# Copying the next expert's first weights ahead of the residual sum, and issuing the weight transfers from the fourth attention step on

## The chip, the cores and the metric

The kernel runs on one core of one Trainium2 chip. The metric is device time in microseconds (us) of one execution. A difference of about 2% is what a measurement of this kernel can tell from none.

## The reference

Attention in chunks of 32 queries feeds a layer of eight experts. Only what matters is shown:

```python
# attention: B, H, S, D = 4, 8, 768, 64; per chunk of 32 queries: 8 memory keys + 16 left + 32 own + 8 right
scores = scale * np.matmul(q_c, k_full.transpose(0, 1, 3, 2))
a = np.exp(scores - np.max(scores, axis=-1, keepdims=True))
a = a / (np.sum(a, axis=-1, keepdims=True) + 1e-09)
out[:, :, c_start:c_end] = np.matmul(a, v_full)
...
# experts: x is [3072, 512]; w1, w2 are [8, 512, 512]
h_dense = np.maximum(x @ w1_dense, 0.0)
y_dense = h_dense @ w2_dense
expert_idx = np.argmax(x @ w_gate, axis=1)
gate_w = probs[np.arange(N), expert_idx]
for e in range(E):
    mask = expert_idx == e
    h = np.maximum(x[mask] @ w1[e], 0.0)
    y_moe[mask] = gate_w[mask, None] * (h @ w2[e])
return (y_dense + y_moe).astype(np.float32)
```

## The kernel before

The work has three stages, one after the other. The instructions of each engine stand in the order in which the code writes them; waits between engines are put in by the framework from the tiles that they share.

**Attention** (loop over `g`, line 392). 24 tiles of 128 queries run through a software pipeline of 28 steps: step `g` does the scores of tile `g`, the transposes of tile `g-1`, the values of tile `g-2` (line 257, reading `vw`), and the gate logits of tile `g-4`. The values come in eight halves of 12 chunks each (`load_v`, lines 139 to 166), many small transfers on SyncE's queue (SP), into three buffers in turn; half `n` serves tiles `3n` to `3n+2`. Queries and keys (`kb`, `qb`, line 135) come by GpSimd's queue (POOL). POOL also casts each tile into its row (line 269) and, once per group of three tiles, scatters the rows to a list per expert in memory, `xs` (line 342). `load_w` (line 75) sends the next of 18 weight transfers on POOL's queue: two for the dense layer, then two for each of eight experts, each 512 KB as it lands in `wall`. Before the change it is called in steps 14 to 27, and four more times in the first steps of the dense stage (line 543).

**Dense stage** (loop at line 540). After a short table of VectorE (DVE) arithmetic, which ends in the row numbers `rowi` (line 466), POOL gathers the 128 tokens of each of 31 slots out of `xs` into `xg` (`fetch`, line 482), three slots ahead. TensorE (PE) transposes them (`turn`, line 492, tile `xt`), and does both dense products: `first` (line 503, 16 matmuls into `ph`, then ReLU into `h` on ScalarE, ACT) and `second` (line 513, four matmuls into `py`). The dense result of a slot is kept in `yds`.

**Expert stage** (loop at line 567). A slot `j` belongs to one expert, whose number is known only at run time. `bring(j)` (line 522) copies that expert's weights to a fixed place: the first weights `wa` on DVE (line 529), half of the second weights `wb` on DVE (line 531) and half on ACT (line 533). Both tiles have two buffers. PE then does `first(j)` with `wa` and `second(j-1)` with `wb`. `finish(j-1)` (line 553) computes the residual sum `o = py * gate + yds` on DVE (line 556) and scatters it to the output on POOL (line 558).

The order in the expert loop is written by hand: PE gets `first(j)`, `second(j-1)`; DVE gets the sum of slot `j-1`, then the copies `wa` and `wb` of slot `j+1`.

Of the kernel before, what the change touches and what calls it, by code (L numbers as in the profile page):

```python
# [11 lines left out]
BF16 = mybir.dt.bfloat16  # L12
# [15 lines left out]
DT, FT = DM // 128, F // 128  # L28
# [4 lines left out]
NSLOT = NT + E - 1  # L33
# [8 lines left out]
def kernel(  # L42
# [14 lines left out]
    nc = tc.nc  # L57
# [9 lines left out]
    wall = const.tile([128, E + 1, DT + FT, 512], BF16, name="wall")  # L67
# [39 lines left out]
    with ExitStack() as one:  # L107
# [75 lines left out]
        def transposes(b, sink):  # L183
            qT = qt_p.tile([128, HP, S], BF16, tag="qT", name=f"qT{b}")
            kbd = kbds[b % 2]

            def step(hp, isk):
                src = qk.pop((b, hp, "kb" if isk else "qb"))
                tp = ps.tile([128, TPB, 128], BF16, tag="ps", name="tp")
                for i in range(TPB):  # L190
                    for par in range(2):
                        nc.tensor.transpose(tp[64 * par:64 * par + 64, i, :],  # L192
                                            src[:, par, D * i:D * i + D], ident,
                                            tile_position=(0, 64 * par))
                tv = tp.rearrange("d i p -> d p i")
                if not isk:
                    nc.scalar.copy(qT[:, hp, :].rearrange("d (p i) -> d p i", i=TPB), tv)
                    load_qk()
                else:
                    for par in range(2):  # L200
                        r = slice(64 * par, 64 * par + 64)
                        dst = kbd[r, hp, par, LEFT:LEFT + S].rearrange("d (p i) -> d p i", i=TPB)
                        nc.scalar.copy(dst, tv[r])  # L203

            for hp in range(HP):
                sink.append(lambda hp=hp: step(hp, True))
                sink.append(lambda hp=hp: step(hp, False))
            return qT, kbd
# [84 lines left out]
        def new_group(n):  # L293
            grp = grps[n]
            grp["row"] = work.tile([128, GRP, ROW], F32, tag="row", name="row")
            grp["pg"] = pg.tile([128, 2, GRP, E], F32, tag="pg", name="pg")
            nc.gpsimd.tensor_copy(
                grp["row"][:, :, DM // 2 + 1].bitcast(I32), tok[:, GRP * n:GRP * n + GRP])
# [93 lines left out]
        for g in range(NT + 4):  # L392
            def do(part, lag):
                if 0 <= g - lag < NT:
                    parts[g - lag][part]()

            if g < NT:
                b, t = divmod(g, TPB)
                if t == 0 and b + 1 < B:
                    steps = []  # L400
                    turned[b + 1] = transposes(b + 1, steps)
                parts[g] = attention(g, *turned[b], grps.setdefault(g // GRP, {}))
            do("scores", 0)
            do("turn", 1)
            if 0 <= g - 2 < NT and (g - 2) % GRP == 0:
                new_group((g - 2) // GRP)
            do("values", 2)
            do("exp", 0)
            if g < NT and t > 0 and steps:
                steps.pop(0)()  # L410
            do("turn_x", 3)
            if g < NT and t > 2 and steps:
                steps.pop(0)()
            do("gate", 4)
            if g >= 14:
                load_w()
            if g % 3 == 1 and g > 3 and g // 3 + 2 < 2 * B:
                load_v(g // 3 + 2)
# [51 lines left out]
    with ExitStack() as two:  # L470
        c2 = two.enter_context(tc.tile_pool(name="c2", bufs=1))
        w2 = two.enter_context(tc.tile_pool(name="w2", bufs=2))
        w3 = two.enter_context(tc.tile_pool(name="w3", bufs=4))
        pt = two.enter_context(tc.tile_pool(name="pt", bufs=2, space=PSUM))
        pf = two.enter_context(tc.tile_pool(name="pf", bufs=3, space=PSUM))
        xTs = c2.tile([128, NSLOT, DT, 128], BF16, name="xTs")
        yds = c2.tile([128, NSLOT, DM], F32, name="yds")
        meta = c2.tile([128, NSLOT, 2], F32, name="meta")

        xgs = {}  # L480

        def fetch(j):
            if j >= NSLOT:
                return
            xg = w3.tile([128, ROW], F32, tag="xg", name="xg")
            nc.gpsimd.indirect_dma_start(  # L486
                xg.bitcast(I32), None, xs[:, :],
                bass.IndirectOffsetOnAxis(ap=rowi[:, j:j + 1], axis=0),
                bounds_check=ZROW, oob_is_err=True)
            xgs[j] = xg  # L490

        def turn(j):
            if j >= NSLOT:
                return
            xg = xgs.pop(j)
            xt = pt.tile([128, DT, 128], BF16, tag="xt", name="xt")
            xb = xg[:, :DM // 2].bitcast(BF16)
            for d in range(DT):
                nc.tensor.transpose(xt[:, d, :], xb[:, 128 * d:128 * d + 128], ident)  # L499
            nc.vector.tensor_copy(xTs[:, j], xt)  # L500
            nc.vector.tensor_copy(meta[:, j, :], xg[:, DM // 2:DM // 2 + 2])

        def first(j, w):
            ph = pf.tile([128, FT, 128], F32, tag="ph", name="ph")
            for f in range(FT):
                for d in range(DT):
                    nc.tensor.matmul(ph[:, f, :], w[:, d, 128 * f:128 * f + 128],  # L507
                                     xTs[:, j, d, :], start=(d == 0), stop=(d == DT - 1))
            h = w2.tile([128, FT, 128], BF16, tag="h", name="h")
            nc.scalar.activation(h, ph, AF.Relu)  # L510
            return h

        def second(h, w):
            py = pf.tile([128, DM], F32, tag="py", name="py")
            for f in range(FT):
                nc.tensor.matmul(py, h[:, f, :], w[:, f, :],  # L516
                                 start=(f == 0), stop=(f == FT - 1))
            return py

        hs, regs, copied = {}, {}, {}  # L520

        def bring(j):

            if j >= NSLOT:
                return
            ev, ea = regs[j]
            wa = w2.tile([128, DT, 512], BF16, tag="wa", name="wa")
            wb = w2.tile([128, FT, 512], BF16, tag="wb", name="wb")
            nc.vector.tensor_copy(  # L529
                wa, wall[:, bass.ds(ev, 1), :DT].rearrange("p a t m -> p (a t) m"))  # L530
            nc.vector.tensor_copy(
                wb[:, :2], wall[:, bass.ds(ev, 1), DT:DT + 2].rearrange("p a t m -> p (a t) m"))
            nc.scalar.copy(  # L533
                wb[:, 2:], wall[:, bass.ds(ea, 1), DT + 2:].rearrange("p a t m -> p (a t) m"))
            copied[j] = (wa, wb)

        for j in range(3):
            fetch(j)
        turn(0)
        for j in range(NSLOT + 1):  # L540
            if j < NSLOT:
                fetch(j + 3)
                load_w()
                hs[j] = first(j, wall[:, E, :DT])
                turn(j + 1)
                regs[j] = (nc.vector.value_load(expi[:1, j:j + 1], min_val=0, max_val=E - 1),
                           nc.scalar.value_load(expi[:1, j:j + 1], min_val=0, max_val=E - 1))
            if j > 0:
                nc.scalar.copy(yds[:, j - 1], second(hs.pop(j - 1), wall[:, E, DT:]))

        sent = []

        def finish(j, wb, h):
            py = second(h, wb)
            o = w3.tile([128, DM], F32, tag="o", name="o")
            nc.vector.scalar_tensor_tensor(o, py, meta[:, j, 0:1], yds[:, j],  # L556
                                           op0=ALU.mult, op1=ALU.add)
            i = nc.gpsimd.indirect_dma_start(  # L558
                out[:, :], bass.IndirectOffsetOnAxis(ap=meta[:, j, 1:2].bitcast(I32), axis=0),
                o, None, bounds_check=NT * 128 - 1, oob_is_err=False)  # L560
            for x in sent:
                tc.declare_no_dep(i.ins, x.ins, reason="different rows of out")
            sent.append(i)

        bring(0)
        bring(1)
        for j in range(NSLOT + 1):
            if j < NSLOT:
                hs[j] = first(j, copied[j][0])
            if j > 0:  # L570
                finish(j - 1, copied[j - 1][1], hs.pop(j - 1))
                bring(j + 1)

# [28 lines left out]
```

## Time and profile before

| what | value |
|---|---|
| three timed runs | 399.64, 406.48, 406.95 us; median 406.48 us |
| the profiled execution | 393.16 us, of which its span is 391.5 us |
| PE busy in the span | 275.8 us (70%) |
| DVE, ACT, POOL busy in the span | 155.9, 169.0 and 147.9 us (40%, 43%, 38%) |
| attention, dense stage, expert stage | until about 201 us; about 208 to 283 us; about 283 us to the end |

All times in the profile are in microseconds from the start of the span, of one execution. An instruction's row gives its start, its length, its engine, its line and its tiles, and in square brackets how long the engine was idle before it and what ended that idle time. PE's matmuls are pipelined: a row of sixteen matmuls shows 1.06 us, while the next group starts 0.89 us after it. PEclk is the granted clock of TensorE: 1.00 is 2.4 GHz, 0.50 is 1.2 GHz.

### The profile page before, as it was taken

The page shows a single profiled execution, that of the slowest core. Times are in us where ns is not written, and L with a number is a line of the kernel's source. Part 1 is how long each engine was busy: PE and PEld are TensorE (multiplying, and loading weights), DVE is VectorE, ACT ScalarE, POOL GpSimd, SP SyncE. Part 2 cuts the span into 40 slices and gives each one's busy share as a digit, 9 for nine tenths or more (in the row PEclk, how much of TensorE's full clock was granted, in tenths as well). Part 3 has the DMA queues.
Part 4 walks back from the last instruction along what each step waited for, and adds up shares of the span by engine and source line. Part 5 has one row for each costly group of instructions (what it writes and reads, how often), then busy time and mean ns, then how long its engine had stood idle before and what let it go on. Part 6 is the DMA issues. An engine that isn't in the chain of part 4 may idle for free.

```text
span 391.5 us, 10333 instructions
## 1 busy us (share of the span) xinstructions
PE 275.8 (70%) x4200; PEld 206.4 (53%) x4200; DVE 155.9 (40%) x432; ACT 169.0 (43%) x253; POOL 147.9 (38%) x183
## 2 busy tenths in 40 slices
PE   2604778788979798889830879999955555555553
PEld 1403567676858576678830657777633333333331
DVE  7104343552444434354352212222435544444553
ACT  3704365364525444233200335555665555444442
POOL 8751321313032231516263845555023333333333
PEclk9999986785556658565555799999999999999999
DMA  8999998995907799875788892223101211221110
GB/s 105 195 188 176 156 172 131 180 153 121 124 32 120 119 141 174 136 105 91 129 139 158 145 199 62 70 70 66 19 28 71 81 64 68 75 79 62 67 59 0
DMA packets 74193, 42.40 MB, mean 108 GB/s; under 512 B 53439, under 2 KB 70848, under 8 KB 74146
## 3 DMA queue, kind: packets, MB, share of 16 engines
q0 software_dynamic: 23616, 29.33, 38.6%
q1 hardware_dynamic: 50530, 12.41, 20.8%
q8 instruction: 33, 0.54, 0.6%
q14 instruction: 14, 0.11, 0.1%
HBM read 48.02 MB, written 11.30 MB: 152 GB/s over the span
## 4 chain that ended last, share of the span: by engine, by line
PE 41%; issue 25%; POOL 10%; DMA 9%; SPq 7%; DVE 4%; ACT 1%; another core or an unknown queue 1%; POOLq 1%; ACTq 0%
POOL out_dram L558 9%; PE xp L257 7%; PE pg L282 7%; PE ph L507 6%; SPq L164 5%; PE xtp L275 5%; PE py L516 5%; PE ap L245 5%; PE tp L192 3%; DMA vw<-in_v_dram 3%; DMA xg<-xs,rowi 3%; DMA vw<-in_mem_v_dram 2%; PE sc L224 2%; SPq L159 2%; DMA xs<-row,si 2%
## 5 line engine op out<-in xcount | busy, mean ns | idle before, releaser
L510 ACT ACTIVATE h<-ph 128x512 bf16<-128x512 f32 x62 | 36.9, 597 | 74.5 <-PE ph L507 73.8
L558 POOL DMA_INDIRECT out_dram<-o,meta x31 | 35.8, 1155 | 78.8 <-DVE o L556 75.2
L507 PE MATMUL ph<-xTs,wa 128*128 128x128 bf16 x496 | 32.9, 220 | 42.0 <-DVE wa L529 42.0
L507 PEld LDWEIGHTS <-wa 128*128 128x128 bf16 x496 | 27.9, 98 | 56.5 <-DVE wa L529 56.3
L269 POOL CAST row<-xn 128x512 bf16<-128x512 f32 x24 | 14.7, 611 | 80.5 <-DVE xn L266 80.5
L556 DVE SCALAR_TENSOR_TENSOR o<-py,meta,yds 128x512 f32<-128x512 f32 x31 | 23.3, 751 | 53.5 <-PE py L516 49.2
L486 POOL DMA_INDIRECT xg<-xs,rowi x31 | 31.8, 1025 | 32.5 <-PE py L516 24.6
L257 PE MATMUL xp<-vw,aT 64*32 64x65 f32 x1536 | 35.8, 294 | 10.6 <-DMA vw<-in_mem_v_dram 5.5
L342 POOL DMA_INDIRECT xs<-row,si x24 | 24.2, 1010 | 34.4 <-DVE mx L233 22.7
L257 PEld LDWEIGHTS xp<-vw,aT 64*32 64x32 f32 x1536 | 24.8, 138 | 22.6 <-issue 18.1
L282 PEld LDWEIGHTS pg<-wgate,x 128*128 128x128 f32 x192 | 35.5, 277 | 1.1 <-issue 0.7
L500 DVE COPY xTs<-xt 128x512 bf16<-128x512 bf16 x31 | 13.2, 425 | 57.2 <-PE xt L499 37.9
L507 PEld LDWEIGHTS <-wall 128*128 128x128 bf16 x496 | 31.3, 100 | 8.2 <-issue 1.4
L245 PE MATMUL ap<-identf,a 128*128 128x128 f32 x96 | 23.6, 392 | 16.9 <-ACT a L240 15.4
L533 ACT COPY wb<-wall 128x1024 bf16 x31 | 32.3, 1045 | 7.4 <-PE py L516 6.7
L282 PE MATMUL pg<-wgate,x 128*128 128x8 f32 x192 | 34.9, 311 | 0.0
L203 ACT COPY kbd<-tp 64x768 bf16<-64x768 bf16 x32 | 25.3, 791 | 21.3 <-PE tp L192 18.0
L507 PE MATMUL ph<-xTs,wall 128*128 128x128 bf16 x496 | 33.8, 223 | 1.0 <-DVE xTs L500 1.0
L516 PE MATMUL py<-wb,h 128*128 128x512 bf16 x124 | 31.7, 379 | 1.3 <-ACT h L510 1.3
L516 PE MATMUL py<-wall,h 128*128 128x512 bf16 x124 | 31.7, 379 | 0.0
L247 ACT COPY aT<-ap 128x512 f32<-128x512 f32 x24 | 14.1, 586 | 39.3 <-PE ap L245 39.0
L516 PEld LDWEIGHTS <-h 128*128 128x128 bf16 x248 | 21.5, 98 | 16.8 <-ACT h L510 2.2
(106 smaller groups left out, 399.5 us busy)
## 6 DMA issues: line engine op xcount, KB each, us to landing
vw<-in_v_dram SPq DMA_DIRECT2D x64, 154.0 KB
wall<-in_moe_w_dram POOLq DMA_DIRECT2D x16, 512.0 KB
kb<-in_k_dram POOLq DMA_DIRECT2D x16, 192.0 KB
qb<-in_q_dram POOLq DMA_DIRECT2D x16, 192.0 KB
vw<-in_mem_v_dram SPq DMA_DIRECT2D x64, 24.0 KB
wall<-in_moe_w_dense_dram POOLq DMA_DIRECT2D x2, 512.0 KB
xg<-xs,rowi POOLq DMA_INDIRECT x31
out_dram<-o,meta POOLq DMA_INDIRECT x31
```

The costliest lines, as they stand in the source:

```text
L203: nc.scalar.copy(dst, tv[r])
L245: nc.tensor.transpose(ap[:, hp, :], st["a"][:, 2 * hp:2 * hp + 2, :], identf)
L257: nc.tensor.matmul(xp[32 * cc:32 * cc + 32, par, (D + 1) * hp:(D + 1) * (hp + 1)], st["aT"][r, hp, 32 * cc:32 * cc + 32], vw[r, hp, 4 * (g ...
L282: nc.tensor.matmul(grp["pg"][:, 0, u, :], st["x32"][:, d, :], wgate[:, d, :], start=(d == 0), stop=(d == DT - 1))
L342: i = nc.gpsimd.indirect_dma_start(xs[:, :], bass.IndirectOffsetOnAxis(ap=si[:, t:t + 1], axis=0), row[:, t, :].bitcast(I32), None, bounds ...
L486: nc.gpsimd.indirect_dma_start(xg.bitcast(I32), None, xs[:, :], bass.IndirectOffsetOnAxis(ap=rowi[:, j:j + 1], axis=0), bounds_check=ZROW, ...
L507: nc.tensor.matmul(ph[:, f, :], w[:, d, 128 * f:128 * f + 128], xTs[:, j, d, :], start=(d == 0), stop=(d == DT - 1))
L510: nc.scalar.activation(h, ph, AF.Relu)
L516: nc.tensor.matmul(py, h[:, f, :], w[:, f, :], start=(f == 0), stop=(f == FT - 1))
L533: nc.scalar.copy(wb[:, 2:], wall[:, bass.ds(ea, 1), DT + 2:].rearrange("p a t m -> p (a t) m"))
L556: nc.vector.scalar_tensor_tensor(o, py, meta[:, j, 0:1], yds[:, j], op0=ALU.mult, op1=ALU.add)
L558: i = nc.gpsimd.indirect_dma_start(out[:, :], bass.IndirectOffsetOnAxis(ap=meta[:, j, 1:2].bitcast(I32), axis=0), o, None, bounds_check=NT ...
```

## The change

Two edits. In the attention loop `load_w` is called from step 3 on, so all 18 transfers are issued in steps 3 to 20 and none is left for the dense stage. In the expert loop `bring` is split into `bring_a` (the copy into `wa`) and `bring_b` (both copies into `wb`); `bring_a(j+1)` now stands ahead of `finish(j-1)`, `bring_b(j+1)` behind it as before.

```diff
             do("gate", 4)
-            if g >= 14:
+            if g >= 3:
                 load_w()
...
-        def bring(j):
-
+        def bring_a(j):
+
+            if j >= NSLOT:
+                return
+            wa = w2.tile([128, DT, 512], BF16, tag="wa", name="wa")
+            nc.vector.tensor_copy(
+                wa, wall[:, bass.ds(regs[j][0], 1), :DT].rearrange("p a t m -> p (a t) m"))
+            copied[j] = [wa]
+
+        def bring_b(j):
             if j >= NSLOT:
                 return
             ev, ea = regs[j]
-            wa = w2.tile([128, DT, 512], BF16, tag="wa", name="wa")
             wb = w2.tile([128, FT, 512], BF16, tag="wb", name="wb")
-            nc.vector.tensor_copy(
-                wa, wall[:, bass.ds(ev, 1), :DT].rearrange("p a t m -> p (a t) m"))
...
-            copied[j] = (wa, wb)
+            copied[j].append(wb)
...
-        bring(0)
-        bring(1)
+        for j in range(2):
+            bring_a(j)
+            bring_b(j)
         for j in range(NSLOT + 1):
             if j < NSLOT:
                 hs[j] = first(j, copied[j][0])
             if j > 0:
+                bring_a(j + 1)
                 finish(j - 1, copied[j - 1][1], hs.pop(j - 1))
-                bring(j + 1)
+                bring_b(j + 1)
```

On DVE, in the middle of the expert stage, the queue before reads as follows (`o` is the residual sum, an `ISA` row sets up the address of the expert):

```order
L556 SCALAR_TENSOR_TENSOR o<-py,meta,yds 128x512
L529 ISA
L529 COPY wa<-wall 128x2048
L531 ISA
L531 COPY wb<-wall 128x1024
L556 SCALAR_TENSOR_TENSOR o<-py,meta,yds 128x512
```

and in the changed kernel, whose line numbers are a little different there:

```order
L527 ISA
L527 COPY wa<-wall 128x2048
L561 SCALAR_TENSOR_TENSOR o<-py,meta,yds 128x512
L536 ISA
L536 COPY wb<-wall 128x1024
L527 ISA
L527 COPY wa<-wall 128x2048
```

The copy into `wa` has moved from behind the sum to the place in front of it; the copy into `wb` stays behind the sum. PE's and ACT's orders are the same in both kernels.

On POOL, early in the attention stage, the queue before reads (`wall` is a weight transfer, `xs` the scatter to the expert lists):

```order
L135 DMA kb<-in_k_dram 128x2x384
L135 DMA qb<-in_q_dram 128x2x384
L269 CAST row<-xn 128x512
L135 DMA kb<-in_k_dram 128x2x384
L135 DMA qb<-in_q_dram 128x2x384
L297 COPY row<-tok 128x3
L269 CAST row<-xn 128x512 x2
L342 DMA xs<-row,si 24577x258 x3
```

and in the changed kernel:

```order
L135 DMA kb<-in_k_dram 128x2x384
L135 DMA qb<-in_q_dram 128x2x384
L78 DMA wall<-in_moe_w_dense_dram 128x4x512
L269 CAST row<-xn 128x512
L135 DMA kb<-in_k_dram 128x2x384
L135 DMA qb<-in_q_dram 128x2x384
L78 DMA wall<-in_moe_w_dense_dram 128x4x512
L297 COPY row<-tok 128x3
L269 CAST row<-xn 128x512
L78 DMA wall<-in_moe_w_dram 128x4x512
L269 CAST row<-xn 128x512
L342 DMA xs<-row,si 24577x258 x3
```

One weight transfer has come in behind each attention step, the first two between the last transfers of queries and keys.

Where the attention stage ends and the dense stage begins, POOL's queue before reads (`xg` is the gather of a slot's tokens):

```order
L269 CAST row<-xn 128x512
L78 DMA wall<-in_moe_w_dram 128x4x512 x2
L342 DMA xs<-row,si 24577x258 x3
L78 DMA wall<-in_moe_w_dram 128x4x512
L486 DMA xg<-xs,rowi 128x258 x4
L78 DMA wall<-in_moe_w_dram 128x4x512
L486 DMA xg<-xs,rowi 128x258
L78 DMA wall<-in_moe_w_dram 128x4x512
```

and in the changed kernel:

```order
L269 CAST row<-xn 128x512 x2
L342 DMA xs<-row,si 24577x258 x3
L269 CAST row<-xn 128x512
L342 DMA xs<-row,si 24577x258 x3
L486 DMA xg<-xs,rowi 128x258 x31
```

No weight transfer is left around the last scatters and the gathers.

## Rows read from the trace of the kernel before

**Rows 1.** Waits of PE in the whole run: total us, times, longest us.

```profile
PE ph L507 <- DVE wa L529: 42.0, 29, 1.5
```

**Rows 2.** Timeline, one slot period of the expert stage: start us, length us, engine.

```profile
322.92 1.07 PE L507 MATMUL ph<-xTs,wa 128*128 128x128 bf16 x16 [1.45 <-DVE wa L529]
...
324.89 0.75 DVE L556 SCALAR_TENSOR_TENSOR o<-py,meta,yds 128x512 f32<-128x512 f32 x1 [1.69 <-PE py L516]
...
325.55 0.68 DVE L529 COPY wa<-wall 128x2048 bf16 x1
325.91 1.17 POOL L558 DMA_INDIRECT out_dram<-o,meta  x1 [2.21 <-DVE o L556]
326.15 0.42 DVE L531 COPY wb<-wall 128x1024 bf16 x1
...
326.30 1.07 PE L507 MATMUL ph<-xTs,wa 128*128 128x128 bf16 x16 [1.45 <-DVE wa L529]
```

**Rows 3.** Timeline, DVE and PE where the expert stage begins.

```profile
282.08 0.42 DVE L531 COPY wb<-wall 128x1024 bf16 x1
282.41 0.69 DVE L529 COPY wa<-wall 128x2048 bf16 x1
...
286.60 1.04 PE L516 MATMUL py<-wb,h 128*128 128x512 bf16 x4 [1.28 <-ACT h L510]
...
289.15 1.07 PE L507 MATMUL ph<-xTs,wa 128*128 128x128 bf16 x16 [1.51 <-DVE wa L529]
```

**Rows 4.** Timeline, PE and POOL at the last slots.

```profile
383.72 1.07 PE L507 MATMUL ph<-xTs,wa 128*128 128x128 bf16 x16 [1.45 <-DVE wa L529]
...
388.00 0.98 POOL L558 DMA_INDIRECT out_dram<-o,meta  x1 [0.30 <-issue]
```

**Rows 5.** The chain that ended last, dense stage: start us, us, what.

```profile
204.98 6.68 DMA xs<-row,si
...
216.42 1.86 PE ph L507 x16
...
219.23 1.26 PE ph L507 x16
...
235.31 0.89 PE ph L507 x16
...
236.43 0.86 PE py L516 x4
```

**Rows 6.** Timeline, the end of the table and the first gather.

```profile
207.50 0.18 DVE L466 TENSOR_SCALAR rowi<-fr 128x31 int32<-128x31 f32 x1
...
212.50 1.08 POOL L486 DMA_INDIRECT xg<-xs,rowi  x1 [5.72 <-DMA xs<-row,si]
```

**Rows 7.** Stretch without weights: busy us of PE, PEld, DVE, ACT, POOL; PEclk, DMA share, GB/s.

```profile
118.00:120.00 2.00, 2.00 (x12) 2.00 (x11) 1.24 (x3) 1.90 (x3) 0.74 (x2) 0.50 0.01 4
```

**Rows 8.** More stretches, same columns: weights nearly alone, two of early attention, expert stage.

```profile
202.00:206.00 4.00, 0.00 (x0) 0.00 (x0) 3.72 (x12) 0.00 (x0) 3.10 (x4) 0.50 1.24 205
...
50.00:58.00 8.00, 5.83 (x191) 4.49 (x188) 3.91 (x9) 5.40 (x9) 2.29 (x5) 0.87 1.35 168
58.00:66.00 8.00, 8.00 (x134) 6.58 (x129) 3.00 (x7) 4.09 (x6) 0.61 (x1) 0.50 0.72 123
...
300.00:380.00 80.00, 45.61 (x471) 28.16 (x468) 39.85 (x71) 39.35 (x48) 26.87 (x25) 1.00 0.19 71
```

**Rows 9.** Timeline, attention: SP's value transfers, PE's value products, a scatter on POOL.

```profile
49.59 1.41 SPq L164 DMA_DIRECT2D vw<-in_mem_v_dram  x1
...
57.68 0.44 PE L257 MATMUL xp<-vw,aT 64*32 64x65 f32 x8 [1.89 <-DMA vw<-in_mem_v_dram]
...
66.35 0.73 SPq L164 DMA_DIRECT2D vw<-in_mem_v_dram  x1
...
77.62 1.19 PE L257 MATMUL xp<-vw,aT 64*32 64x65 f32 x64
...
115.82 0.98 POOL L342 DMA_INDIRECT xs<-row,si  x1 [0.30 <-issue]
```

## Prediction

> **What bounds the kernel now.** I read the waits first. The largest wait of PE by far is for the copy into `wa`: 42.0 us in 29 waits, the longest 1.5 us [rows 1]. These are the slots of the expert stage, so I read one of its periods in the timeline. The reader is to see a closed loop in it [rows 2]. PE starts `first` at 322.92; the sum `o` starts at 324.89, which is 1.97 later, when PE's following `second` is through; the copy into `wa` starts 0.66 after the sum, at 325.55; and PE's next `first` starts 0.75 after the copy, at 326.30. 1.97 + 0.66 + 0.75 = 3.38 us, which is the whole period: PE, the sum and the copy take turns, and PE stands idle for 1.45 us in each. No engine is full: of the 80 us from 300 to 380 PE is busy for 45.61, DVE for 39.85, ACT for 39.35 and POOL for 26.87 [rows 8], which for a period of 3.38 is 1.93, 1.68, 1.66 and 1.14 us.
>
> The chain of the dense stage is the second thing. From the last scatter at 204.98 a transfer holds the chain for 6.68 us, and the eighth `first` (235.31) comes 18.89 us after the first one (216.42), while a slot later on takes 1.98 us (from a `first` at 235.31 to the end of the `second`, 236.43 + 0.86) [rows 5]. The first gather idles 5.72 us for those scatters although `rowi` was ready at 207.50 + 0.18 = 207.68 [rows 6]. Weight transfers run all through this stretch: from 202 to 206 the DMA engines are at a share of 1.24 [rows 8].
>
> **The change, part by part.**
>
> *The copy in front of the sum.* It adds and removes no instruction. It cuts the loop. The copy into `wa` for slot j+1 needs its buffer free, that is, `first(j-1)` done, which is one slot back on PE; so it no longer waits for PE's `second` of the present slot. What is late next? DVE still runs in order: sum j-1, `wb` j+1, `wa` j+2, and `first(j+2)` needs that `wa`. From a sum to the `wb` copy behind it are 0.66 us (the distance sum to copy [rows 2]), from `wb` to the next `wa` 0.33 (282.08 to 282.41 [rows 3]), from there to `first` 0.75, and from `first` to its sum 1.97 [rows 2]. The new loop is 0.66 + 0.33 + 0.75 + 1.97 = 3.71 us, but it spans two slots: 1.86 us a slot. PE alone needs 0.89 + 0.86 = 1.75 us (`first` and `second` in the dense chain, which has transposes beside them [rows 5]). DVE back to back needs 0.66 + 0.33 and a `wa` of some 0.6, about 1.6; ACT the 1.66 above; POOL 1.17 + 0.30 of idle time between two scatters that wait for nothing [rows 2, 4], 1.47. So 1.86 us is the period that I take, with PE's 1.75 as its lower end.
>
> The new order makes nothing else wait. The sum now stands behind `wa`, but that copy is through about 1.68 us after the preceding sum's start (0.66 + 0.33 + 0.69 [rows 2, 3]), before PE has finished the next `second`. The sum also waits for a free `o` out of four buffers; the last scatter is issued from 388.00 to 388.98 and the span ends at 391.5, so a scatter is through at most 2.5 us after its issue, against 4 x 1.86 = 7.4 us.
>
> The count: `first` of slot 2 starts at 289.15 and that of slot 30 at 383.72 [rows 3, 4], 28 periods of 3.38 = 94.57 us. They become 28 x 1.86 = 52.1: 42.5 us less. Slot 2 itself waits 1.51 us for its `wa`; with the copy done earlier it starts behind the `second` that begins at 286.60, at 287.46 (0.86 later): 1.7 less. Together 44.2 us. What follows slot 30 stays.
>
> A rule of the Trainium skill speaks against this. First the rows: a scatter that overlaps copies takes 1.17 us on POOL [rows 2], and the last one, with no copy beside it, 0.98 [rows 4]: 0.19 us for overlapping some 0.65 us of copies. The copy into `wb` that begins in the middle of a scatter takes 0.42 us, the same as where POOL is idle [rows 2, 3]. The page "SBUF — State Buffer", section "Who interferes with whom", says that a DVE copy in its fast mode and a GpSimd instruction lock each other out completely for a whole instruction. The trace doesn't agree with a full lock: by the rows the price is 0.19 us, on an engine with time to spare, and the sum stays; by that page the sum would end at the POOL rival below.
>
> *The weight transfers from step 3 on.* The 18 transfers are the same; they leave the last scatters and the gathers alone. Where scatters have the DMA engines to themselves they land fast: one issued from 115.82 to 116.80 is through by 118, since the share falls to 0.01 after that [rows 7, 9]. So the last scatter, issued by 205.96, is through by about 207.2, and the gather is bound by `rowi`. From the landing at 204.98 + 6.68 = 211.66 to the gather at 212.50 are 0.84 us now [rows 5, 6]; 207.68 + 0.84 = 208.5, so 4.0 us less. Then the first slots: the second `first` comes 2.81 us behind the one at 216.42, for a reason that stays (no `second` covers the transposes yet), and six slots at 1.98 behind it make 14.7 us instead of 18.89: 4.2 less [rows 5]. I take 3.8, for the third slot has little cover too.
>
> What it costs: from 50 to 66 the first three transfers meet the values. A transfer takes 0.524 MB / 205 GB/s = 2.6 us of the DMA engines with little else running [rows 8]. Half 1 of the values is issued until 49.59 + 1.41 = 51.0, and PE waits for its landing at 57.68 [rows 9]; from 50 to 58 the DMA share is already 1.35 [rows 8]. The first weight transfer goes out in step 3, by the order behind the last but one pair of keys and queries, at about that time. At best it queues behind keys and queries and the values keep their turn: 0 us. At worst it and its follower go wholly ahead: 2 x 2.6 = 5.2 us. I take 2, nearer to nothing, since that wait ends 7 us after the values' own issue and most of them are under way by then. Half 2 is issued until 66.35 + 0.73 = 67.1 and first used at 77.62 [rows 9]: more than 9 us of slack against three transfers, 7.8. Later halves have more. From 58 to 66 PE is busy all the time [rows 8], so attention itself goes at PE's pace and hides the rest.
>
> Sum: 44.2 + 4.0 + 3.8 - 2.0 = 50.0 us. Against the profiled execution's own time that is 393.2 - 50 = 343.2 us. The timed runs lie higher, 399.6 to 407.0 with a median of 406.5; the mean of all four executions is 401.6. What makes the difference isn't in the trace, so I set the sum on 404, between mean and median: 354 us.
>
> **The rivals.**
>
> *POOL becomes the bound.* If a scatter can't run at all beside the copies, a slot needs 0.98 + 0.68 + 0.42 + 0.30 = 2.38 us on POOL [rows 2, 4], 28 x 2.38 = 66.6, which is 14.5 more than my 52.1: 368.5 us. It is what the rule of the Trainium skill ("SBUF — State Buffer", "Who interferes with whom") would do here. For it: copies will take 1.10 us of each 1.86. Against it: the 0.19 above.
>
> *The weights' part gives nothing.* The last scatters could be slow for another reason, or the early transfers delay half 1 by the full 5.2 us. The 7.8 us of the dense stage are then lost, and 3.2 more: 365 us. For it: the share of 1.35 at 50 to 58. Against it: the scatter that is through by 118 [rows 7].
>
> *PE alone is the bound.* 28 x 0.11 = 3.1 us less: 351 us. It lies inside my case.
>
> *The values starve: slower than before.* SP's many small value transfers share the DMA engines with one weight transfer a step through steps 3 to 20. If each transfer is paid in full by PE waiting for `vw`, at the rate of a mixed stretch, 123 GB/s [rows 8], it is 4.3 us x 18 = 77 us, against a gain of 52: 404 + 25 = 429 us. It decides against the change where more than 52 / 18 = 2.9 us are lost per transfer. For it: PE waits 1.89 us for values at 57.68 [rows 9]. Against it: the slack of half 2, and PE busy all through 58 to 66.
>
> **How the numbers follow.** My case, PE's bound included, 0.72; POOL's bound 0.12; the weights' part lost 0.12; starving values 0.04, half of it slower, half of it only eating the gain. The low end is the fastest timed run less the full gain, 399.6 - 52 - 3 (PE's bound), and 2 for an execution nearer to the profiled one: 342. The high end takes in both middle rivals, 369. The first three cases are all faster by over 2%: 0.96; the last gives 0.02 for within 2%, about what a measurement of this kernel can tell from no change, and 0.02 for slower.
>
> **What would show it.** Right: the waits list no PE wait for `wa` near 42 us (about 0.1 a slot is left); `first` comes every 1.8 to 1.9 us; scatters on POOL stay at 1.2; the first gather starts about 0.8 us behind `rowi`; eight dense slots take about 15 us. Wrong: POOL back to back with scatters of 1.5 us or more, or DVE copies longer than 0.68 and 0.42; PE waiting for `vw` in the middle of attention; a granted clock under 1.00 in the expert stage, where it is 1.00 now [rows 8] with PE less full than it would be.

## The result, and the profile after

The changed kernel takes 349.4 us in the median of its four executions (348.5 to 360.3). The kernel before has a median of 403.1 us in four (399.6 to 407.0), the three timed ones of above and one more. The ratio is 0.893 [0.879, 0.908]; here and below a ratio compares only the executions in the faster of a kernel's two states, while a median is of all, so the one is not the quotient of the others. The forecast was 354 us. The changed kernel's profiled execution is one of the four, 348.52 us with a span of 346.8; the profiled one of before was 393.16 with a span of 391.5, shorter than all its timed ones.

The two spans differ by 44.7 us. Four distances, each between two rows of the traces, add up to that:

| stretch | before, us | after, us | difference |
|---|---|---|---|
| start of the span to `rowi` ready | 207.68 | 212.45 | +4.8 |
| `rowi` ready to first gather | 4.82 | 1.21 | -3.6 |
| first gather to `first` of slot 0 of the expert stage | 70.87 | 68.07 | -2.8 |
| that `first` to the end of the span | 108.13 | 65.07 | -43.1 |

Nearly everything came from the expert stage; what the weight transfers won behind attention, they lost again inside it.

The waits of the changed kernel in the whole run (total us, times, longest us), to be held against [rows 1]:

```profile
PEld L507 <- DVE wa L527: 12.0, 28, 0.6
...
PE xp L257 <- DMA vw<-in_mem_v_dram: 10.6, 6, 5.0
```

No line of PE itself waiting for `wa` is left. The weight loader still waits for it a little in each slot, 12.0 us in 28 times, beside PE's `second`. The second line, attention waiting for its values, has a longest wait of 5.0 us; that is the loss of the early transfers.

Two slots of the expert stage in the timeline (start us, length us, engine, line, operation), for [rows 2]:

```profile
291.57 1.07 PE L507 MATMUL ph<-xTs,wa 128*128 128x128 bf16 x16
291.59 0.75 DVE L561 SCALAR_TENSOR_TENSOR o<-py,meta,yds 128x512 f32<-128x512 f32 x1
...
292.25 0.42 DVE L536 COPY wb<-wall 128x1024 bf16 x1
...
292.59 0.69 DVE L527 COPY wa<-wall 128x2048 bf16 x1
292.67 1.45 POOL L563 DMA_INDIRECT out_dram<-o,meta  x1 [0.30 <-DVE wb L536]
...
293.34 1.06 PE L507 MATMUL ph<-xTs,wa 128*128 128x128 bf16 x16
293.54 0.75 DVE L561 SCALAR_TENSOR_TENSOR o<-py,meta,yds 128x512 f32<-128x512 f32 x1 [0.27 <-PE py L516]
...
294.21 0.42 DVE L536 COPY wb<-wall 128x1024 bf16 x1
...
294.54 0.69 DVE L527 COPY wa<-wall 128x2048 bf16 x1
294.57 1.51 POOL L563 DMA_INDIRECT out_dram<-o,meta  x1 [0.45 <-DVE o L561]
...
295.29 1.07 PE L507 MATMUL ph<-xTs,wa 128*128 128x128 bf16 x16
295.30 0.75 DVE L561 SCALAR_TENSOR_TENSOR o<-py,meta,yds 128x512 f32<-128x512 f32 x1
```

The predicted loop can be read off: sum at 293.54, `wb` 0.67 later at 294.21, `wa` 0.33 later at 294.54, `first` 0.75 later at 295.29. From the `first` at 291.57 to the sum at 293.54 are 1.97 us. The loop is 3.72 us over two slots, from the `first` at 291.57 to the one at 295.29; a slot takes 1.86 on average, 1.77 and 1.95 in turn. DVE is close behind: it idles 0.27 us ahead of every second sum, and from the sum at 293.54 to the one at 295.30 it goes through sum, `wb` and `wa` without a pause, in 1.76 us.

The first `first` of the stretch that the prediction counted, the last one, and one irregular place in between (same view, for [rows 3, 4]):

```profile
285.84 1.06 PE L507 MATMUL ph<-xTs,wa 128*128 128x128 bf16 x16
...
332.83 0.98 POOL L563 DMA_INDIRECT out_dram<-o,meta  x1 [1.58 <-DVE wa L527]
...
333.43 0.90 DVE L527 COPY wa<-wall 128x2048 bf16 x1
...
337.26 0.75 DVE L561 SCALAR_TENSOR_TENSOR o<-py,meta,yds 128x512 f32<-128x512 f32 x1 [1.19 <-PE ph L507]
...
339.01 1.07 PE L507 MATMUL ph<-xTs,wa 128*128 128x128 bf16 x16
```

339.01 - 285.84 = 53.17 us for 28 periods, where before took 94.57. The excess of 1.1 over 28 x 1.86 = 52.1 lies nearly all at this one place: a scatter starts after an idle time of 1.58, the copy behind it takes 0.90 in place of 0.69, and the sum at 337.26 comes after DVE has been idle for 1.19. It is no chance of one execution: the changed kernel's traces on the third and fourth chip below take 53.1 us for the 28 periods too, and those of the copy's place alone 52.2. Its cause isn't in the rows.

The scatters to the output, by line (busy us, mean ns; then the idle time ahead of them):

```profile
L563 POOL DMA_INDIRECT out_dram<-o,meta x31 | 43.5, 1403 | 28.0 <-DVE o L561 21.9
```

1.40 us on average, 1.155 before. The rows show what it goes with: the rest of the `wa` copy that is under way when a scatter starts. Before, it was 0.32 us (325.55 + 0.68 against 325.91) for a scatter of 1.17 [rows 2]. Now it is 0.61 (292.59 + 0.69 against 292.67) for one of 1.45, and 0.66 (294.54 + 0.69 against 294.57) for one of 1.51.

The way into the dense stage, in the timeline, for [rows 5, 6]:

```profile
212.27 0.18 DVE L466 TENSOR_SCALAR rowi<-fr 128x31 int32<-128x31 f32 x1
...
213.66 1.08 POOL L486 DMA_INDIRECT xg<-xs,rowi  x1 [3.02 <-issue]
...
218.01 1.86 PE L507 MATMUL ph<-xTs,wall 128*128 128x128 bf16 x16 [0.52 <-issue]
...
233.51 1.06 PE L507 MATMUL ph<-xTs,wall 128*128 128x128 bf16 x16
```

The gather starts 1.2 us after `rowi` is ready, where it took 4.8. The eighth `first` comes 15.5 us after the first one. Before, it took 18.7, from 216.42 to this row of the timeline:

```profile
235.15 1.06 PE L507 MATMUL ph<-xTs,wall 128*128 128x128 bf16 x16
```

And the early attention, for [rows 9]:

```profile
50.21 0.78 POOL L78 DMA_DIRECT2D wall<-in_moe_w_dense_dram  x1
...
51.20 1.08 SPq L164 DMA_DIRECT2D vw<-in_mem_v_dram  x1
...
54.67 0.78 POOL L78 DMA_DIRECT2D wall<-in_moe_w_dense_dram  x1
...
57.41 0.35 PE L257 MATMUL xp<-vw,aT 64*32 64x65 f32 x16 [1.75 <-DMA vw<-in_mem_v_dram]
...
62.73 0.44 PE L257 MATMUL xp<-vw,aT 64*32 64x65 f32 x8 [4.96 <-DMA vw<-in_mem_v_dram]
```

The first two weight transfers are issued just before half 1 of the values is wanted, and PE waits 1.75 and 4.96 us in tile 3, where it had waited 0.24 and 1.89. Half 1 is issued until 51.20 + 1.08 = 52.28, and PE has the last of it at 62.73, 10.5 us later; before, it was 6.7 us (51.00 to 57.68 [rows 9]).

### The profile page after: what moved, and what is told of

Read it like the earlier page. It is cut to its first block, busy times and chain, and to the rows that moved or that the text cites. A ratio compares the mean times of both kernels' runs of the same rounds, so it can differ in the third digit from the quotient of the medians.

```text
span 346.8 us, 10305 instructions
## 1 busy us (share of the span) xinstructions
PE 270.2 (78%) x4178; PEld 205.6 (59%) x4200; DVE 156.2 (45%) x432; ACT 167.5 (48%) x253; POOL 155.0 (45%) x183
## 3 DMA queue, kind: packets, MB, share of 16 engines
q0 software_dynamic: 23616, 29.33, 43.1%
## 5 line engine op out<-in xcount | busy, mean ns | idle before, releaser
L563 POOL DMA_INDIRECT out_dram<-o,meta x31 | 43.5, 1403 | 28.0 <-DVE o L561 21.9
L245 PE MATMUL ap<-identf,a 128*128 128x128 f32 x96 | 22.9, 384 | 16.8 <-ACT a L240 15.4
L516 PE MATMUL py<-wb,h 128*128 128x512 bf16 x114 | 29.6, 379 | 2.7 <-ACT h L510 2.2
L516 PE MATMUL py<-wall,h 128*128 128x512 bf16 x112 | 30.1, 379 | 0.6
```

Of the source, the lines that this page charges most:

```text
L245: nc.tensor.transpose(ap[:, hp, :], st["a"][:, 2 * hp:2 * hp + 2, :], identf)
L516: nc.tensor.matmul(py, h[:, f, :], w[:, f, :], start=(f == 0), stop=(f == FT - 1))
L563: i = nc.gpsimd.indirect_dma_start(out[:, :], bass.IndirectOffsetOnAxis(ap=meta[:, j, 1:2].bitcast(I32), axis=0), o, None, bounds_check=NT ...
```

## The experiments

Three things were open: whether the copy's place alone makes the gain, and by the loop that I gave; what the transfers' part is worth by itself; and what the early transfers do to attention. Each group of four runs was on another chip, each time beside the kernel before: the first four on a second chip, the next four on a third, the last four on a fourth. The changed kernel itself was run on the first, third and fourth. Times are compared within a chip only, since before itself has medians of 403.1, 373.8, 397.8 and 394.9 us on the four.

### The two parts apart (second chip)

The copy's new place with the old times of the transfers, in the changed kernel:

```diff
-            if g >= 3:
+            if g >= 14:
                 load_w()
```

> Only the copy is moved; the weight transfers stay in steps 14 to 27 and the dense stage. Theory (the two stages are worth what the two traces show: the expert stage 43 us, the weights 3.6 + 2.8 gained at the dense stage and 4.8 lost in early attention): the span is that of the changed kernel plus 1.6, some 348 us, and the slot period is 1.86 us. Rival (the weights' part is worth the 7.8 us forecast for the dense stage, and the later table was chance): some 354 us of span.

Measured: 325.1 us (320.3 to 331.1) against 373.8, ratio 0.868 [0.854, 0.881]. The 28 periods take 52.2 us, as the loop demands. The span, 318.6 us, is some 30 below both values expected, which were taken over from the first chip.

The transfers alone, in the kernel before:

```diff
-            if g >= 14:
+            if g >= 3:
                 load_w()
```

> Only the weight transfers are moved; the expert loop is that of the kernel before. Theory: the slot period stays 3.38 us, the span is 1.6 us shorter than the 391.5 of before, some 390, which no timing can tell from no change; PE waits 5 us for values of tile 3 and the first gather comes about 1.2 us behind rowi. Rival (7.8 us gained, the early wait was chance): some 384 us, and no wait of 5 us.

Measured: 386.4 us (382.8 to 387.2), ratio 1.040 [1.031, 1.049]. By itself the second edit makes the kernel slower on this chip, by 12.6 us. The windows of the attention stage in both kernels show where (stretch, its length, busy us of PE, PEld, DVE, ACT, POOL, then PEclk, DMA share, GB/s). With the transfers from step 14:

```profile
60.00:170.00 110.00, 97.81 (x2224) 83.31 (x2219) 58.45 (x174) 54.70 (x92) 42.20 (x58) 0.76 0.92 157
```

and from step 3, the stretch being longer because attention is:

```profile
60.00:198.00 138.00, 123.27 (x2250) 103.65 (x2247) 59.64 (x177) 56.74 (x93) 47.29 (x64) 0.57 0.87 154
```

Nearly the same number of matmuls keeps PE busy for 123.27 us in place of 97.81, at a granted clock of 0.57 in place of 0.76. `rowi` comes at 206.40, not at 178.88, 27.5 us later: most of that is PE's own slower work (25.5); its waits for values grow from 2.2 to 9.3 us between 56 and 200.

SP's rows show how the fetching of the values slows down. In the kernel with transfers from step 14, two consecutive halves of the values start to be issued at

```profile
79.70 0.28 SPq L155 DMA_DIRECT2D vw<-in_v_dram  x1
...
90.58 0.82 SPq L152 DMA_DIRECT2D vw<-in_v_dram  x1
```

and in the one with transfers from step 3 at

```profile
94.74 0.28 SPq L155 DMA_DIRECT2D vw<-in_v_dram  x1
...
116.39 0.33 SPq L152 DMA_DIRECT2D vw<-in_v_dram  x1
```

10.9 us apart there, 21.7 here. These two are the closest there: over the last five halves the starts are 13.4 us apart on average (67.34 to 121.09), and 20.6 here (73.80 to 156.02), for three tiles each, which is the pace of attention in that run. PE then waits at the first tiles of later halves too (timeline of the kernel with the transfers alone):

```profile
97.96 0.35 PE L257 MATMUL xp<-vw,aT 64*32 64x65 f32 x16 [1.54 <-DMA vw<-in_mem_v_dram]
...
178.99 0.47 PE L257 MATMUL xp<-vw,aT 64*32 64x65 f32 x16 [1.33 <-DMA vw<-in_mem_v_dram]
```

These rows don't say which came first, the slow halves or the slow PE, since a half is only fetched when PE has left a buffer.

The transfers two steps later, in the changed kernel:

```diff
-            if g >= 3:
+            if g >= 5:
                 load_w()
```

> The changed kernel with the weight transfers from step 5 to step 22. Theory (the first two transfers went ahead of the values of half 1): PE's wait for tile 3 falls from 5.0 to about 1.9 us as before the change, rowi is ready some 4 us earlier, the span is about 342.5 us against 346.8. Rival (that wait was chance, or half 2 then pays instead): no earlier rowi, 347 us, or a new wait for values at tile 6.

Measured: 336.9 us (334.8 to 341.7), ratio 0.911 [0.901, 0.921], 11.8 us slower than the copy's place alone, with intervals well apart. The wait in tile 3 becomes two, of 2.78 and 0.96 us, and 7.7 us of waits for values in the pipeline's stretch from 56 to 200 remain, 4.0 of them in later tiles. `rowi` starts at 199.54 at a clock of 0.62: between the other two. Moving the start by two steps moves the waits and doesn't remove them.

A third buffer for `wa`, which should break the predicted loop and leave PE as the bound:

```diff
-            wa = w2.tile([128, DT, 512], BF16, tag="wa", name="wa")
+            wa = w2.tile([128, DT, 512], BF16, tag="wa", name="wa", bufs=3)
...
+        bring_a(2)
...
-                bring_a(j + 1)
+                bring_a(j + 2)
```

> The changed kernel with three buffers for wa, each copy made one slot earlier. Theory (the 1.86 us are the loop sum, wb, wa, first, second over two slots): the loop then spans three slots, 1.24 us a slot, and PE's own 1.76 is the bound: 28 x 0.1 = 2.8 us less, and PE's matmuls follow each other without a gap. Rival (POOL, with scatters of 1.41 to 1.51 and 0.30 between them, or DVE is the bound): the period stays at 1.8 to 1.86, no change of more than 1 us.

Measured: 336.5 us (335.6 to 342.0), ratio 0.908 [0.900, 0.916], like the run with transfers from step 5 and for the same reason: attention. The expert stage did what the loop demands. Its timeline:

```profile
303.20 1.06 PE L507 MATMUL ph<-xTs,wa 128*128 128x128 bf16 x16
303.40 0.75 DVE L561 SCALAR_TENSOR_TENSOR o<-py,meta,yds 128x512 f32<-128x512 f32 x1
...
304.10 1.03 PE L516 MATMUL py<-wb,h 128*128 128x512 bf16 x4
...
304.49 1.45 POOL L563 DMA_INDIRECT out_dram<-o,meta  x1 [0.31 <-DVE wb L536]
...
304.96 1.06 PE L507 MATMUL ph<-xTs,wa 128*128 128x128 bf16 x16
305.16 0.75 DVE L561 SCALAR_TENSOR_TENSOR o<-py,meta,yds 128x512 f32<-128x512 f32 x1
...
306.25 1.45 POOL L563 DMA_INDIRECT out_dram<-o,meta  x1 [0.30 <-DVE wb L536]
```

From `first` to `first` 1.76 us with `second` in between 0.86 ahead of the next: PE without a gap. POOL is as full, 1.45 of scatter and 0.31 of idle time, and so is DVE: from sum to sum 1.76 (303.40 to 305.16), with no idle time ahead of any of its operations. From `first` of slot 2 to that of slot 30 are 49.2 us, where the changed kernel needs 53.2. So the loop through `wa` was what set 1.86. That PE alone sets 1.76, as the theory has it, isn't shown: all three engines are full at it.

### The same, where attention is slow anyway (third chip)

The changed kernel itself, once more:

> The changed kernel itself, beside the next run, since the first four runs were on another chip than the two traces. Theory (in the runs of e2 to e4 PE waited for values at tiles 9, 12, 18 and 21, because the early weight transfers lengthen the loading of each half to some 20 us; the move of the copy alone is the whole gain): the changed kernel is 10 to 14 us longer than the copy moved alone on a chip where the copy alone runs near 325, and 0 to 6 us longer where it runs near 350. Rival (the weights' move gains the 3.6 + 2.8 less 4.8 that the first two traces show): 1 to 2 us shorter.

Measured: 348.1 us (343.0 to 358.0) against 397.8, ratio 0.882 [0.868, 0.896]. And the copy's place alone, as in the first experiment:

> Only the copy is moved, the weight transfers in steps 14 to 27 and the dense stage: the same program as e1_order_only, to stand beside the run before it. Theory: 325 or 350 us by the chip, no wait for values after tile 3. Rival: 1 to 2 us longer than the changed kernel.

Measured: 350.7 us (346.5 to 355.2), ratio 0.891 [0.880, 0.901]. Here the transfers' part makes no difference that the times can tell: the changed kernel's median is 2.6 us lower, where 0 to 6 us more were expected, and the intervals overlap. Attention in both, first the changed kernel, then the copy's place alone (columns as above):

```profile
60.00:203.00 143.00, 122.75 (x2254) 100.92 (x2255) 59.52 (x177) 57.22 (x93) 47.48 (x64) 0.61 0.93 150
```

```profile
60.00:198.00 138.00, 122.42 (x2213) 98.70 (x2214) 58.51 (x174) 54.83 (x91) 43.05 (x59) 0.60 0.76 125
```

PE is busy equally long at the same low clock. The 5 us between the stretches are waits: 6.8 us for values with the early transfers (5.2 of them in one wait in tile 3), 1.4 without.

A fourth buffer for the values, with less room for keys and queries in exchange, in the changed kernel:

```diff
-QKB = 9
+QKB = 6
...
-        NV = 3
+        NV = 4
...
+        load_v(3)
...
-            if g % 3 == 1 and g > 3 and g // 3 + 2 < 2 * B:
-                load_v(g // 3 + 2)
+            if g % 3 == 1 and g > 3 and g // 3 + 3 < 2 * B:
+                load_v(g // 3 + 3)
```

> The changed kernel with four value buffers instead of three (six instead of nine buffers for queries and keys make the room), so that each half is asked for one half earlier. Theory A (each half comes too late because it is asked for late): PE's waits for values after tile 3 vanish and attention ends as early as without the early weights. Theory B (with all the weights in it attention is bound by what the DMA engines can move: some 28 MB by the last scatter at about 165 GB/s, 170 us): the waits only move, attention ends within 5 us of the changed kernel's.

Measured: 343.6 us (338.4 to 357.2), ratio 0.867 [0.854, 0.881]. In its trace no wait for values is left from 56 to 200 (one of 3.04 us at 53.63 is the last), and `rowi` starts at 203.68, 7.9 us sooner than in the changed kernel beside it; the intervals of the times overlap. But most of that isn't the later halves' doing. The last value product of tile 0, well ahead of the first weight transfer, in the changed kernel and in this one:

```profile
43.03 0.44 PE L257 MATMUL xp<-vw,aT 64*32 64x65 f32 x8 [0.36 <-DMA vw<-in_mem_v_dram]
```

```profile
37.69 0.44 PE L257 MATMUL xp<-vw,aT 64*32 64x65 f32 x8 [0.52 <-DMA vw<-in_mem_v_dram]
```

5.3 us are won there already. The wait of 3.04 us at 53.63 is that of tile 3, which comes ahead of 56 here; it was 5.2 us and another of 1.6. The edit has two parts, and with six buffers in place of nine only 20 of the transfers of keys and queries are issued in the first 31 us, not 26. Whether that part gives the early 5.3 us isn't shown; no run has it alone. So the run doesn't decide between theories A and B. Since the changed kernel has its waits in tile 3 alone on this chip, the run can't show what a fourth buffer would do to the later waits of the second chip. That stays open.

The 18 transfers thinned out, eight in every other attention step from 10 to 24 and ten in every other dense slot from 4 to 22:

```diff
-            if g >= 3:
+            if 10 <= g <= 24 and g % 2 == 0:
                 load_w()
...
-                load_w()
+                if 4 <= j <= 22 and j % 2 == 0:
+                    load_w()
```

> The copy moved; eight weight transfers in the even steps 10 to 24 of attention, the other ten in slots 4 to 22 of the dense stage, one in every second slot. Theory (attention is bound by the DMA engines when it carries all the weights, and the dense stage has them idle): attention no longer than with the copy alone, the first gather 1.2 us behind rowi, no PE wait for a gather, about 8 us less than the copy alone. Rival (weights among the gathers cost as before, 0.6 to 1.0 us of PE wait each): the gain is 4 us or less.

Measured: 350.6 us (343.2 to 355.4), by the median as the copy's place alone; the result has no ratio. The 8 us didn't come, and the rival holds. Now the gathers wait. One of three such rows in the timeline of its dense stage, the others being of 0.81 and 0.96 us:

```profile
266.10 0.40 PE L499 MATMUL xt<-ident,xg 128*128 128x128 bf16 x4 [1.40 <-DMA xg<-xs,rowi]
```

From the first gather to the first scatter of the output are 77.2 us, 76.4 with the copy's place alone and 73.5 in the changed kernel. Transfers among the gathers cost what early ones cost in attention.

### Before once more, and the best of both (fourth chip)

The kernel before, one profiled execution, for its attention on this chip:

> The kernel before, for its attention stage on the chip of the next three runs. Theory (the chips differ in attention: where PE waits some 5 us for instructions, its granted clock there is 0.6 with any order of transfers; where it doesn't, it is 0.76 unless early weights make it wait for values): about 0.6 with issue waits near 5 us and rowi ready near 207 us, or about 0.75 without them and rowi near 180 us. Rival (the early part of a run is chance): neither pairing.

Measured: 390.4 us; `rowi` starts at 204.27, the clock in attention (60 to 196) is 0.65, waits for values take 2.4 us and PE stands 4.5 us in "issue" between 56 and 200. This is the first of the theory's two pairings.

The changed kernel:

> The changed kernel beside the next two. Theory: where the kernel before is near 374 us, 335 to 340; where it is near 398, 348. Rival: 325 on the first kind of chip, as with the copy alone.

Measured: 352.7 us (344.7 to 360.2) against 394.9, ratio 0.885 [0.872, 0.897].

Changed kernel, four value buffers and three for `wa` (the two edits above), transfers from step 3:

> The changed kernel with four value buffers (six for queries and keys) and three wa buffers: the two gains of the runs before together. Theory: the waits for values after tile 3 are gone (6 to 10 us less than the changed kernel) and the slot period is 1.76 (3 us less): 9 to 13 us less than the changed kernel. Rival (the two gains are the same time, or the values' waits return at later tiles): 4 us or less.

Measured: 344.8 us (339.0 to 357.2), ratio 0.876 [0.864, 0.888], 7.9 us under the changed kernel's median, which is between theory and rival; the intervals overlap. Here too attention is ahead from the start, by 5.0 us at the last value product of tile 0 (38.21 against 43.17), and tile 3 still waits 5.02 us.

The same with the transfers from step 14:

```diff
-            if g >= 3:
+            if g >= 14:
                 load_w()
```

> The same with the weight transfers in steps 14 to 27 and the dense stage. Theory: on a chip whose attention has a granted clock near 0.6 it is 4 to 6 us longer than the run before it, since the last scatters and the gathers wait for weights again; on the other kind it is within 6 us of it, for attention then pays for early weights in the clock. Rival: the weights' place makes no difference once the values have four buffers.

Measured: 343.1 us (335.0 to 349.4), ratio 0.863 [0.849, 0.876]. It beats before clearly and has the best median of its chip, 9.6 us under the changed kernel's, though the two intervals still touch. Of these, 5.5 us are there at the last value product of tile 0 (37.65 against 43.17). Between early and late transfers the times show no difference. Attention in the two, early ahead of late (one window of each):

```profile
60.00:203.00 143.00, 126.56 (x2216) 104.20 (x2217) 58.68 (x175) 55.08 (x91) 50.14 (x68) 0.56 0.90 152
```

```profile
60.00:191.00 131.00, 115.97 (x2147) 95.68 (x2132) 56.81 (x172) 53.65 (x89) 47.33 (x64) 0.60 0.82 135
```

The profiled executions differ more than the medians do, by 5.4 us in their spans (342.0 and 336.6), and one execution of each doesn't settle it.

## Why the prediction was right, and where it wasn't

**The copy in front of the sum: right in mechanism and size.** Forecast were 52.1 us for the 28 periods, by a loop over two slots; measured 53.2, with the loop's four distances each as predicted to 0.01 us and 1.1 us lost at one irregular place. Of the 44.2 us, 43.1 came. That the loop sets the period, and not DVE's or POOL's work, is shown by the third `wa` buffer: 1.76 us. DVE's own work was put too low, though, at about 1.6 us: back to back it takes 1.76, so it was only 0.1 from being the bound itself. The granted clock in the expert stage stayed at 1.00 (288 to 340). The copy's place alone gives 0.868 [0.854, 0.881] on the second chip and 0.891 [0.880, 0.901] on the third.

**"Scatters on POOL stay at 1.2": wrong.** They grew to 1.40 on average, 1.45 to 1.51 in the regular slots. It cost nothing, because 1.45 + 0.30 = 1.75 still lies under 1.86; with three `wa` buffers POOL is as full as PE, so no more is to be had from that stage by buffers alone. The step that failed is the price of "0.19 us for overlapping some 0.65 us of copies". It was put on both copies together, and the rows put it on one: a scatter takes 0.98 us, plus the rest of the `wa` copy under way at its start, less 0.13. A rest of 0.32 gives 1.17 [rows 2], 0.61 gives 1.45, and 0.66 gives 1.51. Moving the copy has moved the scatter's start from the middle of the `wa` copy to its beginning. So a scatter waits until that copy is through. This is the lock that the Trainium skill states on its page "SBUF — State Buffer" in the section "Who interferes with whom", which I had called not in agreement with the trace. For a whole scatter the other way round it is not what the rows show: a `wb` copy that starts 0.24 us into a scatter takes 0.42 [rows 2], as without one, and one `wa` copy that starts 0.60 into a scatter takes 0.90 in place of 0.69. The rival of POOL as the bound, at 2.38 us a slot, added scatter and both copies whole, and didn't come: POOL's 0.98 + 0.61 - 0.13 + 0.30 is 1.76.

**The gather and the dense slots: right, a little small.** 3.6 us came of 4.0, and 2.8 of 3.8. The row at 218.01 shows what the second term missed: `first` takes 1.86 us there, not 1.06, and so does the second one at 220.82. Both run at a granted clock of 0.50 (218 to 222), so the second dense slot is as slow as the first; before, the clock was 1.00 from 220 on, in the second `first`. Another 0.2 us of the term was a reading: it took the eighth `first` from the chain at 235.31, and in the timeline it starts at 235.15.

**The early transfers: the term that failed.** I bounded their cost by 0 and 5.2 us and took 2, "nearer to nothing, since that wait ends 7 us after the values' own issue and most of them are under way by then". Measured on the first chip: 4.8 us to `rowi`, with waits in tile 3 that grew from 2.1 to 6.7 us, by 4.6, nearly the bound of two transfers going wholly ahead. That nearly all of half 1 was issued ahead of the transfers didn't help it: the first one went out at 50.21, half 1 was issued by 52.28, and its last part landed at 62.73. With -3.6 and -2.8 behind it, the second edit is worth 1.6 us in the profiled executions of the first chip. By the same mark, the first scatter of the output, it is 2.2 on the third chip (288.70 to 286.51) and 1.5 on the fourth (286.00 to 284.46). No times here can tell that from nothing. My rival "the weights' part gives nothing" came true in the second of its two conditions: attention gave back what was won behind it. Its price of 11 us was too high, since it counted the 7.8 us of the dense stage as lost as well, and 6.4 of them came.

**"Attention itself goes at PE's pace and hides the rest": true only on some chips.** On the first and third chips the early transfers lengthen attention by their wait in tile 3, and PE's own busy time stays (122.25 and 122.80 us from 60 to 199 and 60 to 204 on the first). On the second chip attention without them ran at a clock of 0.76 with 97.8 us of busy PE, and with them at 0.57 with 123.3. There the rival of starving values, to which I gave 0.04, came in part: 12 us slower by the times, not the 77 of its price, and not by waits alone.

**The sum.** Forecast 50.0, measured 44.7 between the profiled executions: the four terms together are 5.3 too high, the early transfers 2.8 of it. The predicted time lies within 5 us all the same because of a second error of the other sign. I had added 11 us for timed runs that lie above the profiled execution; the changed kernel's profiled execution, 348.52, is no more than 1 us below its median. So the mechanism of the main term is no luck, but how near the whole comes is.

**What stays open.** What lowers the granted clock of attention isn't shown. With three `wa` buffers and early transfers PE waited most for values on the second chip (19.8 us from 56 to 200) at a clock of 0.69; with the transfers alone it waited 9.3 us at 0.57. So waits for values don't order the clocks, nor does the DMA share, 0.92 beside the clock of 0.76 and 0.87 beside 0.57.

## What to carry to other kernels

Where engines take turns, follow one buffer round the loop and count over how many slots it closes: moving one copy ahead of an in-order wait turned a loop of 3.38 us over one slot into one of 3.72 over two, and its length was right to 0.01 us before it was run. A transfer that is moved out of one stage's way lands in another's, so price it in the new place at the upper bound first, above all where it meets many small transfers whose consumer is near. And a gain in one part of an edit doesn't vouch for the other part: one run of each alone, on more than one chip, showed that here only one of the two carries the result.

## What the runs showed of the hardware that I had not expected

The chips differ in one stage and not in the others: the 28 periods of the copy's place alone take 52.2 us on the second and on the third. Before's medians run from 373.8 us on the second chip to 403.1 on the first, and the mean granted clock of its timed runs is higher on the second, 0.861 in the median against 0.814 and 0.819 on the third and fourth. In the traces the difference is in attention: on the first, third and fourth chips PE stood 3.7 to 6.6 us in "issue" ahead of its value products between 56 and 200, and the clock there was 0.56 to 0.65, whatever the order of transfers; on the second chip it stood 0 to 1.7 us, and the clock was 0.57 to 0.76. The two go together on the chips seen; that one causes the other isn't shown, and with the transfers alone the second chip had a clock of 0.57 with no such "issue" at all. A trace of before on the second chip was not taken.

A change can therefore have another sign on another chip. Early transfers cost about 12 us on the second chip, in two pairs of kernels (from step 3 and from step 5), and nothing that the times could tell on the third, nor on the fourth with the edited buffers. Each chip was measured at one time only.

A scatter waits for the copy. In the 14 traces here, 431 of the 434 scatters to the output last 0.98 us, plus what is left of the `wa` copy at their start, less 0.13, to within 0.07 us (and 0.98 where 0.13 us or less is left). In the other three the scatter keeps its 0.98, and the `wa` copy that began 0.02 to 0.03 us ahead of it takes 0.75 in place of 0.69. What else in a scatter keeps a copy waiting isn't worked out here.
